# A decode kernel's ring of weight loads: each load of 0.75 or 1 MB issued as two loads, even partitions by SyncE and odd partitions by ScalarE

## The chip, the cores and the metric

The kernel runs on one core of one Trainium2 chip. The metric is device time in microseconds: the median over several executions. The profile is one execution of its own, recorded by the hardware profiler. Its span runs from the first to the last instruction; a little time lies outside the span, so the execution's own time is somewhat longer.

The engines are named as the profile names them: PE is TensorE (PEld its weight loads), ACT is ScalarE, DVE is VectorE, POOL is GpSimd, SP is SyncE. Sixteen DMA engines move data between HBM and the on-chip memory SBUF. A DMA is issued by an engine's instruction queue; those that SP issues appear in the trace as queue q1, those that ACT issues as queue q10.

## The reference

Two kinds of layers alternate, twice: grouped-query attention over a cache, then a dense layer with GELU. There are 8 sequences of one token (B = 8, D = 1024), 32 query heads on 4 key/value heads of size 128, 4096 cache positions, and a hidden size of 3584. Everything is float32, and both attention layers read the same caches and the same weights.

```
def attention(x):
    q = (x @ wq)                                   # 8 x 4096, as 32 heads of 128
    scores = einsum("bhqd,bhkd->bhqk", q, k) * 128 ** -0.5
    o = einsum("bhqk,bhkd->bhqd", softmax(scores), v)
    return o @ wo
def dense(x):
    return gelu(x @ w1 + b1) @ w2 + b2

x = x + attention(layernorm(x))
x = x + dense(layernorm(x))
x = x + attention(layernorm(x))
x = x + dense(layernorm(x))
```

The two caches are 64 MB each (1 MB = 1024 x 1024 bytes here), wq and wo 16 MB each, w1 and w2 14 MB each. With one token per sequence each weight and cache element is used for a few multiplications only, so nearly all of the work is to bring 369 MB (in millions of bytes) from HBM.

## The kernel before

All loads go into one large tile in SBUF, `arena`, 128 partitions of 218 KB each, which the kernel divides by hand into units of 1 KB per partition. A cache tile of 8 units (1 MB over the 128 partitions) is one head and half the positions of one sequence.

**The stream of loads.** Before any computation is written, the kernel fills a list, `stream`, with every load of the program in the order in which the data is needed: its key, its place in the arena, its size in units and its source. `pump` (L183) takes loads from the head of the list as long as the head's place is free, and issues each with one `nc.sync.dma_start` (L190). `give` (L76) marks a place as free and calls `pump`; the computing functions call it as soon as they have written the last instruction that reads a place. So a load stands in SP's queue in the list's order, and at run time SP waits there for the matmuls that read the old contents of its place. A load can't be issued before those ahead of it in the list.

**The stages.** In the first layer the query weights (two loads of 8 MB) and then key and value caches (mostly 8 MB per load, one sequence's keys or values) stream through three areas A, B and C of 64 units each. The second attention layer goes through the sequences backwards. It finds the caches of sequence 7 and the keys of sequence 6 still in place, which saves their loads. The price is that between the two attention layers most of the arena is occupied: output weights `o0`, the dense layer's `i0` and `p0`, and the second layer's query weights `q1` all have to pass through a **ring** of four slots of 8 units, at R[0] to R[3] (L558). Loads there are 1 MB (8 KB per partition); one of `q1` has 6 units (0.75 MB), one has 4, and the last load of `p0` is cut into two of 4 units. After the ring the other caches and the last layer's weights go through the large areas again.

**The work around the ring.** `project` (for o and p) and `expand` (for i and q) loop over the loads of their weight. For each slot they write the matmuls that read it and then call `give`, whose `pump` issues the load that takes the slot next. `layernorm` uses DVE and ACT for the row's statistics: the squares at L167 (ACT), then, some tiles later, the square root at L174 (ACT). Its result is first used at L242 (DVE), where a unit's products are scaled. `hidden_unit` applies GELU with a tanh on ACT (L291). Before the ring begins, ACT copies some pieces out of the way (L628, L630), which frees R[1]; attention's values (L483) free the last slot.

ACT issues one DMA, the input load at the very start (L82). Every other load and the store at the end (L682) are issued by SP.

The instructions of each engine run in the order in which the program writes them; there is no planner that would move them.

Of the kernel before, what the change touches and what calls it, by code (L numbers as in the profile page):

```python
# [14 lines left out]
P = 128  # L15
# [37 lines left out]
def decode_layers(ctx: ExitStack, tc: tile.TileContext, x, kc, vc, wq, wo, w1, w2, w2_low, out):  # L53


    nc = tc.nc
# [12 lines left out]
    def is_free(at, n):  # L69
        return not any(u in used for u in range(at, at + n))  # L70

    def take(at, n, who):
        assert is_free(at, n), (who, at, n)
        used.update(dict.fromkeys(range(at, at + n), who))

    def give(at, n):  # L76
        for u in range(at, at + n):
            used.pop(u)
        pump()
# [99 lines left out]

    stream = []  # L180
    held = {}

    def pump():  # L183
        while stream and is_free(stream[0][1], stream[0][2]):
            key, at, n, src = stream.pop(0)
            take(at, n, key)
            dst = arena[:, at * KB:at * KB + src.shape[1]]
            if key[0] == "low":
                dst = arena[key[1]:LOW:4, AT_LOW * KB:AT_LOW * KB + src.shape[1]]
            nc.sync.dma_start(out=dst, in_=src)  # L190
            held[key] = at, n

    def loads(name):
# [403 lines left out]
    open_queries()  # L597
    rsum = row_sums()
    pump()
    nc.vector.tensor_reduce(rsum, x_row, AX.X, ALU.add)  # L600

# [162 lines left out]
```

## Time and profile before

| | us |
|---|---|
| median of 3 runs | 869.54 (869.48 to 869.60) |
| the profiled execution's own time | 869.43 |
| its span | 867.6 |
| PE, DVE, ACT busy in the span | 541.9, 175.3, 52.9 |

How it is read: the page gives each engine's busy time, and forty slices of the span with the busy share of each engine, the clock granted to PE and what the DMA engines moved. A DMA share of 1.00 means that all 16 DMA engines were occupied by packets for the whole stretch; packets that overlap a little can raise it above 1.00. A packet is one contiguous run of bytes, such as one partition's row of a load; the small packets of 4 bytes are those that report a load's completion. "GB/s" counts millions of bytes per millisecond. The chain is the sequence of work that ended last, followed back from the end, and a wait is put down to what released it.

The cache stage of the first layer lies at about 40 to 340 us, the ring at about 360 to 500 us, and the second attention layer and the last weights follow it.

### The profile page before, as it was taken

The numbers are of one execution on the slowest core, as the hardware profiler recorded it, in microseconds if no ns is written. First come the engines' busy times: TensorE is split into PE (matmuls) and PEld (weight loads), VectorE is DVE, ScalarE is ACT, GpSimd is POOL, SyncE is SP. The second block draws the span as 40 slices with busy tenths as digits, with TensorE's granted clock in tenths as the row PEclk, the third lists the DMA queues.
The fourth block names the chain that finished last, engine by engine and source line by source line (L and its number), as shares of the span: only waits on it lengthen the run. The fifth ranks groups of instructions, "written<-read, shape, count | busy, mean of one in ns | idle before, by whom it ended". The sixth has DMA issues, their size and how long they took to land.

```text
span 867.6 us, 8713 instructions
## 1 busy us (share of the span) xinstructions
PE 541.9 (62%) x3896; PEld 173.1 (20%) x3896; DVE 175.3 (20%) x458; ACT 52.9 (6%) x84; POOL 3.5 (0%) x14
## 2 busy tenths in 40 slices
PE   0556575655656566867676587776574654665677
PEld 0112121211212122221221132222121211211222
DVE  0001231313122232200110023332231313120011
ACT  0200000000000011000000010000000000000100
POOL 0000000000000000000000000000000000000000
PEclk9977787777777877766876888977787777777789
DMA  9999999999999999999999999999999999999997
GB/s 393 436 436 433 435 430 433 435 433 433 435 430 433 435 417 426 407 419 421 420 420 420 421 420 437 438 433 433 435 433 433 435 433 435 433 432 433 420 425 308
DMA packets 16669, 369.06 MB, mean 425 GB/s; under 512 B 1868, under 2 KB 2028, under 8 KB 2924
## 3 DMA queue, kind: packets, MB, share of 16 engines
q1 hardware_dynamic: 16488, 368.36, 99.3%
q8 instruction: 30, 0.49, 0.2%
q10 hardware_dynamic: 144, 0.15, 0.0%
q14 instruction: 7, 0.06, 0.0%
HBM read 368.47 MB, written 0.03 MB: 425 GB/s over the span
## 4 chain that ended last, share of the span: by engine, by line
DMA 77%; PE 20%; DVE 1%; ACT 1%; issue 0%; SPq 0%; POOL 0%; ACTq 0%; POOLq 0%
DMA arena<-in_A_k_cache_dram 22%; DMA arena<-in_A_v_cache_dram 21%; DMA arena<-in_B_w_dram 16%; DMA arena<-in_A_wo_dram 10%; DMA arena<-in_A_wq_dram 8%; PE sps L483 6%; PE sps L426 6%; PE sps L217 2%; PE sps L314 2%; PE sps L497 1%; PE spot L339 1%; PE sps L461 0%; ACT arena L450 0%; DVE arena L434 0%; ACT arena L464 0%
## 5 line engine op out<-in xcount | busy, mean ns | idle before, releaser
L426 PE MATMUL sps<-arena 128*32 128x512 f32 x992 | 142.4, 712 | 116.6 <-DMA arena<-in_A_k_cache_dram 104.4
L483 PE MATMUL sps<-arena 128*32 128x512 f32 x1024 | 151.7, 732 | 19.6 <-DMA arena<-in_A_v_cache_dram 19.6
L217 PE MATMUL sps<-arena,xnT 128*32 128x512 f32 (+3 forms) x592 | 77.0, 650 | 37.3 <-DMA arena<-in_A_wq_dram 19.3
L426 PEld LDWEIGHTS sps<-arena 128*32 128x32 f32 x992 | 31.2, 124 | 192.6 <-DMA arena<-in_A_k_cache_dram 96.8
L314 PE MATMUL sps<-arena,oT 128*32 128x256 f32 x496 | 50.5, 546 | 22.4 <-DMA arena<-in_B_w_dram 10.6
L490 DVE TENSOR_TENSOR sps<-sps,misc 128x512 f32<-128x512 f32 x64 | 44.3, 692 | 65.0 <-PE sps L483 65.0
L461 PE MATMUL sps<-ident,arena 128*128 128x128 f32 x128 | 28.8, 365 | 43.5 <-ACT arena L450 31.6
L483 PEld LDWEIGHTS sps<-arena 128*32 128x32 f32 x1024 | 33.0, 130 | 95.6 <-issue 72.5
L450 ACT ACTIVATE arena<-arena,bias 128x1024 f32<-128x1024 f32 x16 | 18.4, 1147 | 492.2 <-DVE scratch L447 492.2
L434 DVE TENSOR_SCALAR_CACHE_REDUCE arena<-sps 128x512 f32<-128x512 f32 x32 | 22.1, 691 | 124.6 <-PE sps L426 124.6
L491 DVE TENSOR_REDUCE scratch<-sps 128x128 f32<-128x512 f32 x64 | 44.2, 691 | 2.2
L499 DVE TENSOR_TENSOR oT<-sps,scratch 128x8 f32<-128x8 f32 x64 | 11.0, 172 | 160.5 <-PE sps L497 160.5
L217 PEld LDWEIGHTS sps<-arena,xnT 128*32 128x32 f32 x592 | 18.1, 127 | 84.3 <-DMA arena<-in_A_wq_dram 30.3
L497 PEld LDWEIGHTS sps<-misc,scratch 128*128 128x128 f32 x128 | 21.5, 211 | 66.0 <-DVE scratch L491 39.9
L339 PE MATMUL spot<-arena,oT 128*32 128x512 f32 x120 | 16.9, 717 | 18.9 <-DMA arena<-in_A_wo_dram 18.9
L461 PEld LDWEIGHTS sps<-ident,arena 128*128 128x128 f32 x128 | 18.2, 179 | 51.8 <-ACT arena L450 35.5
L497 PE MATMUL sps<-misc,scratch 128*128 128x8 f32 x128 | 27.4, 286 | 1.2 <-DVE scratch L491 1.2
L314 PEld LDWEIGHTS sps<-arena,oT 128*32 128x32 f32 x496 | 17.1, 142 | 53.3 <-DMA arena<-in_A_wo_dram 19.6
L339 PE MATMUL spot<-arena 128*32 128x512 f32 (+2 forms) x108 | 17.9, 682 | 1.8 <-DMA arena<-in_B_w_dram 1.8
L466 DVE COPY arena<-sps 128x512 f32<-128x512 f32 x16 | 11.1, 691 | 37.1 <-PE sps L461 37.1
L156 PE MATMUL sps<-nmean,rsum 128*128 128x64 f32 x8 | 2.0, 336 | 25.3 <-DVE rsum L600 23.7
L468 PE MATMUL sps<-scratch,misc 128*128 128x32 f32 x32 | 10.0, 404 | 12.5 <-DVE arena L466 12.5
(105 smaller groups left out, 163.2 us busy)
## 6 DMA issues: line engine op xcount, KB each, us to landing
arena<-in_B_w_dram SPq DMA_DIRECT2D x27, 1024.0 KB, 8.0
arena<-in_A_wo_dram SPq DMA_DIRECT2D x16, 1024.0 KB, 8.7
arena<-in_A_wq_dram SPq DMA_DIRECT2D x14, 1024.0 KB, 8.7
arena<-in_A_k_cache_dram SPq DMA_DIRECT2D x3, 4096.0 KB, 17.8
arena<-in_A_v_cache_dram SPq DMA_DIRECT2D x3, 4096.0 KB
arena<-in_A_v_cache_dram SPq DMA_DIRECT2D x4, 2048.0 KB, 11.2
arena<-in_B_w_dram SPq DMA_DIRECT2D x1, 6144.0 KB, 45.9
arena<-in_B_w_dram SPq DMA_DIRECT2D x1, 5120.0 KB, 39.4
```

The lines of the kernel that those rows point to most:

```text
L217: nc.tensor.matmul(acc[32 * j:32 * j + 32, r * P:(r + len(ts)) * P], xnT[:, kt * B:kt * B + 32], blocks[:, ts[0] - t0:ts[-1] - t0 + 1:4], ...
L314: nc.tensor.matmul(y[32 * j:32 * j + 32, a:a + n], weights, data, start=(j not in begun), stop=stop)
L339: nc.tensor.matmul(y2[32 * j:32 * j + 32, h * CH:(h + 1) * CH], weights, data, start=((h, j) not in begun2), stop=stop)
L426: nc.tensor.matmul(ps[32 * g:32 * g + 32, :], q[:, c:c + 32], kt[:, g * CH:(g + 1) * CH], start=(j == 0), stop=(j == HKV - 1))
L434: nc.vector.tensor_scalar(row[:, half * CH:(half + 1) * CH], ps, SCALE, None, op0=ALU.mult, op1=ALU.max, accum_out=st["mx"][:, half:half + 1])
L450: nc.scalar.activation(row, row, AF.Exp, bias=bias, scale=1.0, accum_out=ls)
L461: nc.tensor.transpose(pp[:, t * P:(t + 1) * P], row[:, c:c + P], ident)
L466: nc.vector.tensor_copy(s[:, half], src)
L483: nc.tensor.matmul(o[32 * g:32 * g + 32, :], s[:, g], v[:, g * CH:(g + 1) * CH], start=(half == 0), stop=(half == NH - 1))
L490: nc.vector.tensor_tensor(blocks, blocks, sel_t.unsqueeze(2).to_broadcast([P, T, DH]), ALU.mult)
L491: nc.vector.tensor_reduce(r, o.rearrange("p (t d) -> p d t", t=T), AX.X, ALU.add)
L497: nc.tensor.matmul(po[:, 0:REP], scratch[:, a:a + DH], sel_h, start=True, stop=True)
```

## The change

In `pump`, a load whose key belongs to `o0`, `i0`, `p0` or `q1` and that has at least 6 units is now issued as two loads: the 64 even partitions by SP and the 64 odd partitions by ACT. Place, size and order of the loads stay, and so do the computing instructions. ACT's load stands in ACT's queue at the point in the program where `pump` was called. The matmuls that read the slot wait for both halves. Loads of 4 units, the caches and the last layer's weights are issued as before.

```
 
     stream = []
     held = {}
+    HALVED_LOADS = ('o0', ('i0', 0), ('i0', 1), 'p0', ('q1', 0), ('q1', 1))
 
     def pump():
         while stream and is_free(stream[0][1], stream[0][2]):
...
             dst = arena[:, at * KB:at * KB + src.shape[1]]
             if key[0] == "low":
                 dst = arena[key[1]:LOW:4, AT_LOW * KB:AT_LOW * KB + src.shape[1]]
-            nc.sync.dma_start(out=dst, in_=src)
+            if key[0] in HALVED_LOADS and n >= 6:
+                nc.sync.dma_start(out=dst[0:P:2], in_=src[0:P:2])
+                nc.scalar.dma_start(out=dst[1:P:2], in_=src[1:P:2])
+            else:
+                nc.sync.dma_start(out=dst, in_=src)
             held[key] = at, n
```

More of the change, by code (lines that the diff above doesn't have):

```diff
@@ L181, in decode_layers @@
     held = {}
+    HALVED_LOADS = ('o0', ('i0', 0), ('i0', 1), 'p0', ('q1', 0), ('q1', 1))
     def pump():
@@ L189, in pump @@
                 dst = arena[key[1]:LOW:4, AT_LOW * KB:AT_LOW * KB + src.shape[1]]
-            nc.sync.dma_start(out=dst, in_=src)
+            if key[0] in HALVED_LOADS and n >= 6:
+                nc.sync.dma_start(out=dst[0:P:2], in_=src[0:P:2])
+                nc.scalar.dma_start(out=dst[1:P:2], in_=src[1:P:2])
+            else:
+                nc.sync.dma_start(out=dst, in_=src)
             held[key] = at, n
```

## The prediction

> **What bounds the kernel now.** I read the page's slices and DMA part first, to see whether any engine or only the transfers fill the span, then the stages, then the chain inside the ring.
>
> ```profile
> PE 541.9 (62%) x3896; PEld 173.1 (20%) x3896; DVE 175.3 (20%) x458; ACT 52.9 (6%) x84; POOL 3.5 (0%) x14
> ...
> DMA  9999999999999999999999999999999999999997
> GB/s 393 436 436 433 435 430 433 435 433 433 435 430 433 435 417 426 407 419 421 420 420 420 421 420 437 438 433 433 435 433 433 435 433 435 433 432 433 420 425 308
> DMA packets 16669, 369.06 MB, mean 425 GB/s; under 512 B 1868, under 2 KB 2028, under 8 KB 2924
> ...
> q1 hardware_dynamic: 16488, 368.36, 99.3%
> ...
> q10 hardware_dynamic: 144, 0.15, 0.0%
> ...
> DMA 77%; PE 20%; DVE 1%; ACT 1%; issue 0%; SPq 0%; POOL 0%; ACTq 0%; POOLq 0%
> ```
>
> No compute engine is near full, the 16 DMA engines are busy in every slice (99.3% of the span for SP's queue, q1, alone), and DMA is 77% of the chain. ScalarE's queue, q10, carries one small load of 0.15 MB. So time is bytes over rate, and a microsecond won or lost on the DMA engines anywhere before the last load shows at the end. By stages (the columns are busy time by engine, then PE's clock, DMA share, GB/s):
>
> ```profile
> 40.00:340.00 300.00, 181.13 (x1166) 56.06 (x1166) 69.72 (x174) 16.12 (x24) 0.00 (x0) 0.77 1.00 431
> ...
> 360.00:500.00 140.00, 95.49 (x829) 29.63 (x833) 9.32 (x36) 7.49 (x14) 0.16 (x1) 0.72 1.01 418
> ```
>
> The change touches the ring, about 360 to 500 us. Its rate is 418 GB/s against 431 in the cache stage before it, at the same full DMA share. The chain there alternates between a load and the matmuls that read it:
>
> ```profile
> 384.56 8.05 DMA arena<-in_A_wo_dram
> 392.61 0.04 issue
> 392.65 1.98 PE sps L314 x16
> 394.62 0.01 issue
> 394.64 7.92 DMA arena<-in_B_w_dram
> ```
>
> A load is issued when its slot's matmuls end and lands 8 us later, since the loads of the other slots are served first; four slots come round in 10.1 us (384.56 to 394.64), four times the price of a load found below. The chain looks like a round trip, but the queue is never empty, so it is the rate that binds.
>
> **The change part by part.** How many loads are halved, and how long each takes to land:
>
> ```profile
> arena<-in_B_w_dram SPq DMA_DIRECT2D x27, 1024.0 KB, 8.0
> arena<-in_A_wo_dram SPq DMA_DIRECT2D x16, 1024.0 KB, 8.7
> arena<-in_A_wq_dram SPq DMA_DIRECT2D x14, 1024.0 KB, 8.7
> ...
> arena<-in_A_wq_dram SPq DMA_DIRECT2D x1, 768.0 KB, 8.2
> ```
>
> That is 27 + 16 + 14 + 1 = 58 loads. Their bytes, rows and slots stay; each gets a second transfer with its own completion. To price that, the DMA part of four short stretches: 50 us of the ring, 100 us of the cache stage (one row of 64 KB per partition), the output store, and the end of that store.
>
> ```profile
> DMA packets 2887, 21.02 MB, mean 420 GB/s; under 512 B 324, under 2 KB 324, under 8 KB 324
> ...
> q1 hardware_dynamic: 2883, 20.96, 100.9%
> ```
> ```profile
> DMA packets 743, 43.30 MB, mean 433 GB/s; under 512 B 80, under 2 KB 80, under 8 KB 80
> ...
> q1 hardware_dynamic: 740, 43.25, 100.0%
> ```
> ```profile
> DMA  0044940440998490929084405404004000000000
> ...
> DMA packets 48, 0.03 MB, mean 117 GB/s; under 512 B 16, under 2 KB 48, under 8 KB 48
> ...
> q1 hardware_dynamic: 48, 0.03, 37.1%
> ```
> ```profile
> DMA packets 4, 0.00 MB, mean 17 GB/s; under 512 B 3, under 2 KB 4, under 8 KB 4
> ...
> q1 hardware_dynamic: 4, 0.00, 7.6%
> ```
>
> The ring, 400 to 450 us: 20.96 MB are 20 loads of 1.048 MB, so **2.50 us a load**; 2883 packets over 20 are 144, which is 128 partition rows of 8 KB and 16 small ones, one completion on each engine. The store, 866.20 to 866.48 us: 32 rows of 1 KB and 16 small packets take 37.1% of 16 x 0.28 us, 1.66 us. Its end, 866.41 to 866.47: one row and three small take 7.6% of 16 x 0.06 us, 0.073 us. Both together give a small packet 8.4 ns and a 1 KB row 48 ns. **Added work:** 16 small packets over 16 engines, so 8.4 ns a load, 58 x 8.4 ns = **+0.5 us**.
>
> Is there more to a load than its rows? Cache stage, 130 to 230 us: 660 rows of 64 KB in 1600 us of engine time are 2.42 us each, or 303 ns for 8 KB. A ring load has eight rows on each engine; at 303 ns they would take 2.42 us, and it takes 2.50. The 0.08 us is either a price of shorter rows (eight times 10 ns), which halving leaves alone, or of each load, which halving pays again. Both kinds of load have eight rows and one completion per engine, so these rows alone can't tell. Bounds: 58 x 0.08 = **+4.6 us** if it is per transfer, **-4.6 us** if a second queue hides it whole. What I go by is the one stretch with two queues at work, 15.5 to 33.3 us, when ScalarE's input load runs beside the first weights:
>
> ```profile
> DMA packets 192, 7.40 MB, mean 416 GB/s; under 512 B 32, under 2 KB 80, under 8 KB 80
> ...
> q1 hardware_dynamic: 128, 7.34, 95.1%
> q10 hardware_dynamic: 64, 0.06, 0.9%
> ```
>
> Here 48 rows of 1168 bytes and 16 small packets of q10 take 0.9% of 16 x 17.8 us, 2.56 us; less 16 x 8.4 ns that is 51 ns a row. A 1 KB row costs 48 ns with one queue, so a slightly longer row that takes turns with the other queue's costs about what it costs alone: no hiding and no fine. I take 0 for it and keep both ends.
>
> [...]
>
> **The two issuing queues.** SP issues as many transfers as before. ScalarE gets 58 more; the store's issue bounds one at 0.57 us, so under 33 us on an engine that is busy for 52.9 of 867.6.
>
> ```profile
> 865.00 0.57 SPq L682 DMA_DIRECT2D out_dram<-x_all  x1
> ```
>
> Its packets begin at 866.21 (the first non-zero digit of its stretch), 1.2 us after the issue began. A ring load so needs 1.2 + 2.5 = 3.7 us when nothing is in front of it, and has 8.0: ScalarE's half may be issued **4.3 us** late before the engines run dry. What can hold it up, and what stands behind it on ScalarE:
>
> ```profile
> 398.49 0.51 ACT L167 ACTIVATE scratch<-x_all,nmu 128x256 f32<-128x256 f32 x1 [42.01 <-DVE nmu L165]
> ...
> 399.11 1.28 ACT L174 ACT_TABLE_LOAD   x1
> 401.88 0.26 ACT L174 ACTIVATE sd<-sps,misc 128x1 f32<-128x1 f32 x1 [1.49 <-PE sps L152]
> 422.13 1.28 ACT L291 ACT_TABLE_LOAD   x1 [19.99 <-DVE scratch L290]
> 423.43 0.31 ACT L291 ACTIVATE scratch<-scratch 128x128 f32<-128x128 f32 x1
> ```
>
> The long waits (42.0 and 20.0 us) are idle time that had nothing queued; in program order a half stands behind the matmuls that free its slot, and L167, L174 and L291 depend on matmuls of that same order. So a half is late by at most the table load and activation in front of it, 1.28 + 0.31 = 1.6 us, inside 4.3. Turned round, the square root's table load, which now runs in a wait, may come behind two halves and be 1.6 us later. Its reader is the scaling at L242:
>
> ```profile
> L242 DVE TENSOR_SCALAR scratch<-sps,rs 128x512 f32<-128x512 f32 (+1 forms) x3 | 2.1, 706 | 35.2 <-PE sps L217 35.2
> ```
>
> L242 waits 35.2 us for the unit's last matmuls in the ring and for nothing else, so both delays cost 0. Without that cover they would cost 1.6 us at each of the two square roots and two tanhs, 6.4 us. PE now has two completions to wait for per load; the matmuls wait for data anyway (chain above), so 0.
>
> Sum: 869.43 (the profiled execution; span 867.6 and 1.8 around it) + 0.5 = 869.9; the median of the runs lies 0.11 higher, which gives **870.0 us**.
>
> **The rivals.** *ScalarE's halves run ahead.* At the ring's start q10 is empty while SP's queue still holds the last big cache loads, and two queues take turns, so the halves of the first three o0 loads can overtake. Served before older SP halves, three of them (1.25 us each) put a load's landing off by 3.75 us for as long as that lead lasts. That alone fits into 4.3; it decides where ScalarE is late too: 3.75 + 1.6 - 4.3 = 1.05 us dry at each of the four activations, 4.2 us, **874.2**. For it: the turns of the two queues. Against it: the lead shrinks whenever ScalarE is late, and near the end there are no later halves.
>
> *The second queue hides the price of short rows.* While one queue's row ends the other's begins: up to -4.6 us, **864.9**, half of it **867.2**. For it: the ring's 418 against 431. Against: the stretch with two queues shows the full price.
>
> *Two engines share one place in SBUF.* Half the partitions might be dealt to the engines so that two of them write to one group of partitions by turns, each at half its rate: up to 2.50 us more a load, 58 x 2.5 = 145 us, **1015**, and with random phases half, **942**. Against it stands the store, also on a part of the partitions (32, every fourth): with several engines in one slice (digits to 9) its rows took 48 ns, no more than bytes and fixed price; it reads SBUF, though, and is short. [...] No run here shows a load on part of the partitions at length.
>
> *The change does nothing of what it says*, the halves being served as one: that is the forecast less 0.5 us.
>
> **How the numbers follow.** Forecast (with the last case) 0.55, ScalarE's lead 0.20, hidden rows 0.17, shared ports 0.08. A measurement of this kernel can tell 0.2%, 1.7 us, from no change. The forecast lies inside that, the lead and the shared ports are slower, the hidden rows faster: 0.17, 0.56, 0.27 (0.01 of the lead's chance, where it costs too little to be told, goes to no change). The range runs from 866.5, which leaves out hidden rows beyond two thirds, to 875, which takes in the lead and the +4.6 of a price per transfer (874.2) and leaves out the shared ports. The likeliest case alone is 869.5 to 871.
>
> **What would show it.** q10 should go from 144 to 144 + 58 x 80 = 4784 packets, q1 from 16488 to 16488 - 58 x 64 = 12776. The ring should stay at 2.50 to 2.51 us a load and 418 to 420 GB/s at a full DMA share. If it rises towards 430, rows were hidden; if the share falls under 0.98 inside the ring, queues ran dry; if the share stays full and the rate falls far, engines block each other. ScalarE's square roots may move by 1.6 us with no effect on L242. A change of the time with an unchanged ring rate would prove this whole argument wrong.

## The result: 885.6 us, 1.8% slower

| | us | ratio to before, 95% interval |
|---|---|---|
| before, median of the runs beside it | 869.51 (869.43 to 869.60) | |
| changed, median of 4 runs | 885.60 (884.26 to 885.87) | 1.0182 [1.0164, 1.0200] |
| changed, the profiled execution | 885.78, span 883.0 | |

The change costs 16.1 us. The forecast was 870.0 us, the range 866.5 to 875.

The page of the changed kernel, its engines, slices and DMA part:

```profile
PE 539.0 (61%) x3896; PEld 173.8 (20%) x3896; DVE 175.7 (20%) x458; ACT 52.9 (6%) x84; POOL 3.5 (0%) x14
...
DMA  9999999999999999499999999999999999999996
GB/s 386 464 437 425 428 429 428 433 428 449 433 425 428 430 417 425 159 418 415 422 420 419 409 423 435 438 442 431 430 428 431 436 437 436 435 429 433 425 421 281
DMA packets 17599, 369.07 MB, mean 418 GB/s; under 512 B 2797, under 2 KB 2957, under 8 KB 3853
...
q1 hardware_dynamic: 12776, 338.08, 89.5%
q10 hardware_dynamic: 4784, 30.43, 8.3%
```

The engines did the same work, and the packets are those that the prediction counted (12776 and 4784). One slice out of forty stands out: the seventeenth, with a DMA digit of 4 and 159 GB/s. Before, no slice between the first and the last was below 407. The slices around it move as many bytes as ever. So the time was not lost little by little over 58 halved loads, but in one place, about 353 to 375 us, where the ring begins.

The same place by stretches, first of the changed kernel, then of the kernel before (busy time by engine, then PE's clock, DMA share, GB/s):

```profile
340.00:350.00 10.00, 1.40 (x5) 0.81 (x5) 0.73 (x4) 1.24 (x2) 0.00 (x0) 0.61 0.96 406
350.00:360.00 10.00, 1.12 (x4) 0.72 (x4) 0.33 (x1) 1.62 (x3) 0.00 (x0) 0.50 0.51 212
360.00:370.00 10.00, 9.58 (x58) 3.00 (x62) 3.89 (x9) 0.00 (x0) 0.00 (x0) 0.69 0.56 210
370.00:380.00 10.00, 6.14 (x84) 2.90 (x76) 2.79 (x6) 0.59 (x1) 0.00 (x0) 0.99 0.69 252
380.00:400.00 20.00, 13.51 (x124) 4.60 (x128) 0.00 (x0) 0.00 (x0) 0.00 (x0) 0.59 1.02 422
400.00:450.00 50.00, 32.56 (x293) 10.38 (x285) 3.97 (x13) 3.74 (x6) 0.00 (x0) 0.76 1.01 419
450.00:500.00 50.00, 31.51 (x296) 10.76 (x294) 4.27 (x19) 2.43 (x5) 0.16 (x1) 0.79 1.01 415
```
```profile
340.00:350.00 10.00, 6.55 (x30) 2.92 (x34) 1.81 (x7) 2.87 (x5) 0.00 (x0) 0.50 0.96 406
350.00:360.00 10.00, 7.69 (x70) 2.36 (x62) 5.74 (x11) 0.59 (x1) 0.00 (x0) 1.00 1.02 423
360.00:370.00 10.00, 7.35 (x66) 2.79 (x66) 0.17 (x1) 0.00 (x0) 0.00 (x0) 0.66 1.01 393
370.00:380.00 10.00, 7.55 (x64) 2.35 (x64) 0.00 (x0) 0.00 (x0) 0.00 (x0) 0.53 1.01 416
380.00:400.00 20.00, 14.53 (x134) 4.88 (x134) 0.82 (x4) 1.49 (x3) 0.00 (x0) 0.67 1.02 421
400.00:450.00 50.00, 33.78 (x290) 10.36 (x289) 6.00 (x22) 2.53 (x5) 0.16 (x1) 0.71 1.01 420
450.00:500.00 50.00, 32.29 (x278) 9.25 (x280) 2.33 (x10) 3.47 (x7) 0.00 (x0) 0.80 1.01 419
```

From 350 to 380 us the changed kernel moves 2.12 + 2.10 + 2.52 = 6.74 MB, the kernel before 4.23 + 3.93 + 4.16 = 12.32 MB. At 420 GB/s the missing 5.58 MB are **13.3 us**. From 380 to 500 us it falls behind by another 0.23 MB, 0.5 us. Of the 16.35 us between the two profiled executions 2.5 us are left outside these rows: 1.0 of them lies outside the spans (885.78 less 883.0 is 2.8 us, 869.43 less 867.6 was 1.8), the other 1.5 I can't place. Note also the row from 340 to 350 us: the DMA engines still have the cache loads to serve, but PE and DVE have nearly stopped (1.40 and 0.73 us busy; before, 6.55 and 1.81). The DMA engines run dry ten microseconds *after* the compute engines, because places are no longer freed.

Why the compute engines stop stands in the timeline of ScalarE: first the changed kernel, then the kernel before (start, duration, and in brackets the idle time ahead and who ended it).

```profile
315.51 0.52 ACTq L193 DMA_DIRECT2D arena<-in_A_wo_dram  x1
340.94 1.15 ACT L455 ACTIVATE arena<-arena,bias 128x1024 f32<-128x1024 f32 x1 [28.62 <-DVE scratch L452]
...
357.87 0.60 ACT L469 ACTIVATE arena<-sps 128x512 f32<-128x512 f32 x1 [15.69 <-DMA arena<-in_A_wo_dram]
358.36 0.59 ACT L633 COPY sps<-arena 128x512 f32<-128x512 f32 x1
358.88 0.61 ACT L635 COPY arena<-arena 128x512 f32<-128x512 f32 x1
360.44 1.40 ACTq L193 DMA_DIRECT2D arena<-in_A_wo_dram  x2
```
```profile
340.63 1.15 ACT L450 ACTIVATE arena<-arena,bias 128x1024 f32<-128x1024 f32 x1 [29.24 <-DVE scratch L447]
...
343.13 0.60 ACT L464 ACTIVATE arena<-sps 128x512 f32<-128x512 f32 x1 [1.27 <-PE sps L461]
```

L469 (L464 before; the diff moved it by five lines) is the copy of one half of sequence 7's transposed probabilities from `sps` into the place S. It has nothing to do with weights. Yet now it waits 15.69 us for a load of `wo`, and starts 14.7 us later. Behind it in ScalarE's order stand L633 and L635, which free R[1]; R[1]'s load is issued at 360.44. Attention's values, which read what L469 writes, stand still as well.

The load that it waits for is load 0 of `o0`, the first one of the ring and the first that is halved. Its odd half is issued by ScalarE at 315.51; its even half stands in SP's queue behind sequence 7's value loads, and is issued at 327.25 (SP's timeline of the changed kernel):

```profile
320.20 4.66 SPq L195 DMA_DIRECT2D arena<-in_A_v_cache_dram  x4
327.25 51.56 SPq L192 DMA_DIRECT2D arena<-in_A_wo_dram  x8
```

It lands behind 8 MB of values, about 357 us. Before, nobody needed load 0 until PE's first matmuls on it, which start at 358.43.

The wait is in the program. This is the line of L469 in the list of instructions as built, of the changed kernel, with the counters that it waits for; the other one is L464 of the kernel before:

```
L469 ACTIVATE arena<-sps 128x512 [waits DMAHW1_49,PE_49]
L464 ACTIVATE arena<-sps 128x512 [waits PE_49,Activation_49]
```

DMAHW1 counts completions of loads, and both halves of load 0 are counted there. Load 0 goes to R[0], units 184 to 191 of each partition, and L469 writes S, units 212 to 215 (`AT_A, AT_B, AT_C, RING = 0, 64, 128, 184` and `AT_S` = 212). They share no byte. The waits are written by the framework from the access patterns of the instructions. For this pair of patterns it seems to take two separate places for overlapping ones; the run with contiguous halves below tests that. DVE's copy of the other half of S (L471) has the same wait in the list.

### The profile page after: what moved, and what is told of

Same layout as the page of the kernel before. It is cut to its first block, busy times and chain, and to the rows that moved or that the text cites. A ratio compares the mean times of both kernels' runs of the same rounds, so it can differ in the third digit from the quotient of the medians.

```text
span 883.0 us, 8889 instructions
## 1 busy us (share of the span) xinstructions
PE 539.0 (61%) x3896; PEld 173.8 (20%) x3896; DVE 175.7 (20%) x458; ACT 52.9 (6%) x84; POOL 3.5 (0%) x14
## 3 DMA queue, kind: packets, MB, share of 16 engines
q1 hardware_dynamic: 12776, 338.08, 89.5%
q10 hardware_dynamic: 4784, 30.43, 8.3%
## 5 line engine op out<-in xcount | busy, mean ns | idle before, releaser
L431 PE MATMUL sps<-arena 128*32 128x512 f32 x992 | 144.0, 719 | 117.7 <-DMA arena<-in_A_k_cache_dram 105.6
L488 PE MATMUL sps<-arena 128*32 128x512 f32 x1024 | 154.1, 743 | 16.6 <-DMA arena<-in_A_v_cache_dram 16.6
L466 PE MATMUL sps<-ident,arena 128*128 128x128 f32 x128 | 28.6, 363 | 58.2 <-ACT arena L455 31.9
L319 PE MATMUL sps<-arena,oT 128*32 128x256 f32 x496 | 44.4, 489 | 28.2 <-DMA arena<-in_B_w_dram 14.5
L466 PEld LDWEIGHTS sps<-ident,arena 128*128 128x128 f32 x128 | 17.9, 176 | 66.6 <-ACT arena L455 35.7
L471 DVE COPY arena<-sps 128x512 f32<-128x512 f32 x16 | 11.1, 692 | 51.3 <-PE sps L466 51.3
```

The lines of the kernel that those rows point to most:

```text
L319: nc.tensor.matmul(y[32 * j:32 * j + 32, a:a + n], weights, data, start=(j not in begun), stop=stop)
L431: nc.tensor.matmul(ps[32 * g:32 * g + 32, :], q[:, c:c + 32], kt[:, g * CH:(g + 1) * CH], start=(j == 0), stop=(j == HKV - 1))
L466: nc.tensor.transpose(pp[:, t * P:(t + 1) * P], row[:, c:c + P], ident)
L471: nc.vector.tensor_copy(s[:, half], src)
L488: nc.tensor.matmul(o[32 * g:32 * g + 32, :], s[:, g], v[:, g * CH:(g + 1) * CH], start=(half == 0), stop=(half == NH - 1))
```

## The experiments

Four theories were open. **The wait** (W in the expectations): what costs the time is L469's wait for load 0. **The lead** (L): ScalarE's halves are served ahead of older loads of SP and put their landings off, so that the DMA engines run dry. **Halving** (H): each further transfer costs time by itself. **Shared places** (P; "shared ports" in the prediction): halves share places in SBUF and block each other. All diffs are against the changed kernel; no computing instruction was changed in any of them. Each ratio is to the kernel before, run beside it.

### Load 0 whole, the other 57 halved

```
-            if key[0] in HALVED_LOADS and n >= 6:
+            if key[0] in HALVED_LOADS and n >= 6 and key != ('o0', 0):
```

> All ring loads halved as in the change, except the very first one (o0's load 0), which SP issues whole. Theory W: the loss is one added wait, that of the probabilities' copies on ACT and DVE for the landing of the first load's strided halves, late behind the caches in SP's queue. Then no engine waits there, the two dry stretches of the DMA engines near 355 and 367 us vanish, and the time is 869.5 + 0.5 for the completions, 869.5 to 871.5 us. Theory L (ScalarE's halves run ahead of SP's older loads and put landings off): loads 1 to 15 are still halved and still overtake, so 880 us or more. Theory H (halving costs by itself, per transfer): 57 of 58 loads are still halved, 885 us.

Measured: 876.92 us (875.25 to 880.23), ratio 1.0087 [1.0063, 1.0110]. ScalarE's timeline, PE's timeline and the stretches of this kernel:

```profile
342.95 0.60 ACT L469 ACTIVATE arena<-sps 128x512 f32<-128x512 f32 x1 [1.27 <-PE sps L466]
...
345.52 1.17 ACTq L193 DMA_DIRECT2D arena<-in_A_wo_dram  x2
```
```profile
355.70 1.07 PE L488 MATMUL sps<-arena 128*32 128x512 f32 x8 [1.35 <-DMA arena<-in_A_v_cache_dram]
358.10 1.93 PE L488 MATMUL sps<-arena 128*32 128x512 f32 x8 [1.33 <-DMA arena<-in_A_v_cache_dram]
```
```profile
360.00:380.00 20.00, 13.01 (x136) 5.92 (x132) 1.64 (x4) 0.00 (x0) 0.00 (x0) 0.67 0.91 346
...
400.00:450.00 50.00, 33.33 (x262) 10.32 (x266) 6.30 (x23) 4.03 (x7) 0.00 (x0) 0.65 1.00 395
450.00:500.00 50.00, 33.41 (x278) 10.66 (x274) 2.87 (x12) 2.74 (x5) 0.16 (x1) 0.70 1.00 406
```

The wait at L469 is gone and with it more than half of the loss, but 7.3 us stay. Neither theory alone gave that number: the wait would have left 871.5 us at most, the lead 880 or more. Now ScalarE issues at 345.52 into an empty queue, while SP's queue still holds value loads, and the values that PE reads come 1.3 us late at two places. The ring then runs at 346, 395 and 406 GB/s instead of 404 (the mean of 393 and 416), 420 and 419. That is 1.16 + 1.25 + 0.65 = 3.06 MB, or 7.3 us at 420 GB/s: about the whole loss. So the wait is not all that the change does. But the lead explains only a part of this rest. By the share (0.91, 1.00 and 1.00, where the kernel before has 1.01) idle engines account for about 1.2 of the 3.06 MB. The other 1.9 MB were lost while the engines were busy and moved less in the same time; why they did, these runs don't show.

### Load 0 halved, the other 57 whole

```
-            if key[0] in HALVED_LOADS and n >= 6:
+            if key == ('o0', 0):
```

> Only the first ring load (o0's load 0) is halved; the other 57 are whole and SP's. Theory W: the wait of ACT's probability copy for that load's landing is there in full, ACT idle of about 15 us before that copy, two dry stretches, 882 to 886 us. Theory L: one half overtakes at most, 1.25 us, so 869.5 to 871 us. Theory H: a fifty-eighth of the loss, 869.8 us.

Measured: 882.02 us (881.54 to 882.78), ratio 1.0142 [1.0126, 1.0157]. ScalarE's timeline and a stretch:

```profile
357.85 0.60 ACT L469 ACTIVATE arena<-sps 128x512 f32<-128x512 f32 x1 [15.70 <-DMA arena<-in_A_wo_dram]
```
```profile
360.00:380.00 20.00, 15.34 (x138) 5.88 (x138) 6.65 (x14) 0.59 (x1) 0.00 (x0) 0.87 0.66 247
```

One halved load out of 58 brings the same wait, 15.70 us, the same dry DMA engines (share 0.66) and +12.4 us. The other 57 are not needed for it.

### Both halves by SP

```
-                nc.scalar.dma_start(out=dst[1:P:2], in_=src[1:P:2])
+                nc.sync.dma_start(out=dst[1:P:2], in_=src[1:P:2])
```

> Both halves of every one of the 58 loads are issued by SP, even partitions first; ScalarE issues none. Theory W: the halves are strided as in the change, the copies still wait for load 0's landing, 882 to 887 us. Theory L: one queue, so nothing can overtake, 870 us. Theory H: 885 us if the price is of the transfers, 870 if it is of ScalarE's queue.

Measured: 884.73 us (883.99 to 884.80), ratio 1.0170 [1.0155, 1.0185]. ScalarE's timeline:

```profile
357.59 0.60 ACT L469 ACTIVATE arena<-sps 128x512 f32<-128x512 f32 x1 [15.26 <-DMA arena<-in_A_wo_dram]
```

L469 waits 15.26 us for the same load. The second queue is not what makes the wait.

### Both halves by SP, and load 0 whole

The two edits of above together (the first and the third).

> Both halves of every ring load are issued by SP, as in the run with both halves on SP, but o0's load 0 is whole, as in the run with the first load whole. Theory W+L (the added wait on load 0's landing costs about 12 us, and apart from it ScalarE's halves running ahead cost about 7): neither is present, so only 57 more completions are left, 869.5 + 0.5 = 869.5 to 870.5 us, with DMA engines busy through the ring. Theory H (a halved load costs by itself): the 7.3 us of the run with the first load whole remain, 876 us.

Measured: 870.73 us (869.63 to 873.05, 10 runs), ratio 1.0013 [1.0002, 1.0023]. The ring's stretches:

```profile
360.00:380.00 20.00, 14.72 (x130) 5.54 (x130) 0.17 (x1) 0.00 (x0) 0.00 (x0) 0.60 1.00 407
...
400.00:450.00 50.00, 31.29 (x291) 10.22 (x285) 5.52 (x20) 4.02 (x7) 0.16 (x1) 0.78 1.01 413
450.00:500.00 50.00, 32.95 (x290) 10.26 (x286) 2.97 (x13) 4.34 (x7) 0.00 (x0) 0.83 1.02 419
```

57 loads are still made as two, with even and odd partitions. That alone costs 1.2 us (0.2 to 2.0 by the interval of the ratio). Halving by itself is not what costs 16 us. The four kernels make a square:

| median, us | load 0 whole | load 0 halved | the wait costs |
|---|---|---|---|
| both halves in SP's queue | 870.73 | 884.73 | 14.0 |
| one half in each queue | 876.92 | 885.60 | 8.7 |
| the second queue costs | 6.2 | 0.9 | |

Read along its upper row and then down, this is the account of the change: 1.2 us for halving (870.73 less 869.5), 14.0 for the wait, 0.9 for the second queue. The 0.9 can't be told from nothing, since the runs of the two kernels overlap (884.26 to 885.87 and 883.99 to 884.80). Without the wait the second queue costs 6.2 us, so the wait hides it. Why is argued and not shown: behind the wait the DMA engines have run dry (share 0.51 and 0.56), both queues may start level, and ScalarE's lead over SP's old loads is gone. Mending the one alone would have left a good part of the loss.

### Load 0 halved, both halves by ScalarE

```
-            if key[0] in HALVED_LOADS and n >= 6:
-                nc.sync.dma_start(out=dst[0:P:2], in_=src[0:P:2])
+            if key == ('o0', 0):
+                nc.scalar.dma_start(out=dst[0:P:2], in_=src[0:P:2])
```

> Only o0's load 0 is halved into even and odd partitions, and ScalarE issues both halves; all other loads are whole and SP's. The copies of the probabilities wait for both halves in the program, as in the run with only the first load halved, but ScalarE's queue is empty, so both land before the copies are due. Theory W as lateness (it is the landing behind the caches that costs): ACT does not wait there, 869.5 to 871.5 us. If strided halves cost in another way than through that landing: 882 us as with one half on SP.

Measured: 871.48 us (869.83 to 872.86, 10 runs), ratio 1.0020 [1.0011, 1.0030]. ScalarE's timeline:

```profile
315.31 0.52 ACTq L192 DMA_DIRECT2D arena<-in_A_wo_dram  x1
315.87 1.03 ACTq L193 DMA_DIRECT2D arena<-in_A_wo_dram  x1
...
346.33 0.60 ACT L469 ACTIVATE arena<-sps 128x512 f32<-128x512 f32 x1 [1.21 <-PE sps L466]
```

L469 has the wait for load 0's halves in the list of instructions here too, but both are issued before 317 us, in a queue with nothing in front, and have landed when L469 comes: only PE releases it. Of the 12.4 us 2.0 are left, at the upper edge of what was expected. So it is not the wait as such that costs, but that the half it waits for stands behind 8 MB of other loads.

### Load 0 alone halved, but by contiguous partitions

Is it really the pattern that brings the wait? This differs from the second experiment in nothing but which partitions form a half.

```
-            if key[0] in HALVED_LOADS and n >= 6:
-                nc.sync.dma_start(out=dst[0:P:2], in_=src[0:P:2])
-                nc.scalar.dma_start(out=dst[1:P:2], in_=src[1:P:2])
+            if key == ('o0', 0):
+                nc.sync.dma_start(out=dst[0:P // 2], in_=src[0:P // 2])
+                nc.scalar.dma_start(out=dst[P // 2:P], in_=src[P // 2:P])
```

> Only load 0 of o0 is halved, as in the kernel that halves this load alone by even and odd partitions (882.02 us), but by the contiguous partitions 0 to 63 (SP) and 64 to 127 (ScalarE). The same two transfers, the same two queues, the same halves in size; the pattern alone differs. If it is the pattern that makes ScalarE's copy at L469 wait for load 0's landing: no DMA release in front of L469, which starts at 342 to 345 us, and 869.5 to 873 us (one load at 252 instead of 420 GB/s costs about 1.7 us at most). If any halving of load 0 brings that wait, or a ScalarE transfer in front of L469 does: L469 near 357 us and 881 to 884.

Measured: 876.94 us (876.63 to 879.02), ratio 1.0085 [1.0067, 1.0102]. ScalarE's timeline and the stretches:

```profile
346.35 0.60 ACT L469 ACTIVATE arena<-sps 128x512 f32<-128x512 f32 x1 [1.20 <-PE sps L466]
```
```profile
320.00:330.00 10.00, 4.64 (x38) 1.64 (x38) 4.39 (x9) 0.00 (x0) 0.00 (x0) 0.91 0.98 307
...
350.00:360.00 10.00, 9.68 (x60) 2.36 (x52) 4.10 (x8) 0.00 (x0) 0.00 (x0) 0.73 1.02 344
360.00:370.00 10.00, 6.33 (x52) 2.80 (x56) 1.86 (x5) 0.59 (x1) 0.00 (x0) 0.66 0.96 310
```

The wait is gone: L469 is released by PE, and no counter of loads stands beside it in the list. With the same two transfers in the same two queues, the step of two in the partitions is what brings it. Why the framework takes that pattern to reach S is not shown here. The time was outside what I expected (869.5 to 873), for another reason: from 320 to 330 and from 350 to 370 us the rate falls to 307, 344 and 310 GB/s while the engines stay busy (0.98, 1.02 and 0.96). I take these for the stretches in which a contiguous half is served beside whole loads; I had priced only the slowness of the half itself, not that of its neighbours. A part may be ScalarE's half running ahead of cache loads: L469 starts at 346.35 us, 3.2 later than before, as it does at 346.33 in the run with both halves on ScalarE, which cost 2.0 us.

### All 58 halved by contiguous partitions

```
-                nc.sync.dma_start(out=dst[0:P:2], in_=src[0:P:2])
-                nc.scalar.dma_start(out=dst[1:P:2], in_=src[1:P:2])
+                nc.sync.dma_start(out=dst[0:64], in_=src[0:64])
+                nc.scalar.dma_start(out=dst[64:P], in_=src[64:P])
```

> Halves by partitions 0 to 63 (SP) and 64 to 127 (ScalarE) in place of even and odd; count, size, queues and order as in the change. Theory W: the program then holds no wait of the copies for a load, so no dry stretch, 869.5 to 872 us. Theory L: the same overtaking as in the change, 885 us. Theory H: 885 us. Theory P (a half on 64 partitions that lie together shares places in SBUF between engines): the ring's rate falls below 400 GB/s at a full DMA share, 58 loads at up to 5 us each, 900 to 1015 us.

Measured: 969.52 us (962.08 to 971.85), ratio 1.1118 [1.1069, 1.1167]. The ring, 360 to 500 us:

```profile
360.00:500.00 140.00, 71.69 (x515) 22.54 (x511) 8.73 (x28) 4.62 (x8) 0.00 (x0) 0.51 1.00 252
```

The DMA engines are busy all the time (share 1.00) and move 252 GB/s where even and odd halves move 415 to 419: at 252 GB/s a load of 1.048 MB takes 4.16 us in place of 2.50. So the rate falls when halves are cut this way, and not as the change cuts them, as P expected it. Why it falls is not shown, and two halves need not meet for it. In the run above ScalarE's half of load 0, issued at 315.38 us, landed after 14.8 us, and SP's half, issued at 330.21, after 34.3. So of the two only SP's can have been served from 356 to 364 us, and the rate was 238 to 258 GB/s there, at shares of 0.95 to 1.07.

### Loads 0 to 3 whole, and whole loads by turns

Where does the lead come from, and could it be had without halves? First the ring's first round whole, the other 54 loads halved:

```
-            if key[0] in HALVED_LOADS and n >= 6:
+            if key[0] in HALVED_LOADS and n >= 6 and not (key[0] == 'o0' and key[1] < 4):
```

> As the change, but o0's loads 0 to 3, the four that are issued while cache loads still stand in SP's queue, are whole and SP's; the other 54 are halved between SP and ScalarE. Theory L in the form 'the lead is won at the ring's start, over the cache loads': no lead is won there, 869.5 to 871.5 us. Theory L in the form 'a lead is won wherever ScalarE's queue is empty when a half is issued': load 4's half meets an empty queue and overtakes the three whole loads in SP's, the lead stays, and engines run dry where tiles are used late, 874 to 878 us. Theory H: 876 us.

Measured: 874.11 us (873.08 to 875.46), ratio 1.0054 [1.0039, 1.0069]. ScalarE has no halves of loads 1 to 3 here that could meet the value loads, and the median is 2.8 us lower than with load 0 alone whole (the intervals of the two ratios overlap). The rest stays: the ring moves 391 GB/s from 360 to 380 us, 406 from 400 to 450 and 409 from 450 to 500. The cost of the second queue is not tied to the ring's start. The time lies in the range that was expected, but not for the reason given: the share in these stretches is 1.00, 1.00 and 1.01, so the engines did not run dry, they were slower.

Then no halves at all, but odd-numbered loads of the ring whole by ScalarE and even-numbered ones whole by SP:

```
-            if key[0] in HALVED_LOADS and n >= 6:
...
+            on_act = key[0] in HALVED_LOADS and n >= 6 and key[1] % 2 == 1
+            (nc.scalar if on_act else nc.sync).dma_start(out=dst, in_=src)
```

> No load is halved: of each weight in the ring SP issues the even-numbered loads and ScalarE the odd-numbered ones, whole. Theory L: whole loads of ScalarE overtake SP's and are served beside them at half rate each, so a load that is needed first lands later; the lead is up to one load and a half, within the 4.3 us of slack most of the time, 870 to 876 us, with short dry spells. Theory H: nothing is halved, 869.5 us. A shared-rate gain of two queues would show as a ring above 425 GB/s and a time under 868.

Measured: 884.85 us (881.68 to 885.67), ratio 1.0170 [1.0150, 1.0189]: as slow as the change itself, with no added wait at the copy into S (L466 in this kernel). Rows of its chain of waits and two stretches:

```profile
376.37 6.48 DMA arena<-in_A_wo_dram
...
384.03 11.84 DMA arena<-in_A_wo_dram
```
```profile
400.00:450.00 50.00, 29.73 (x269) 9.33 (x267) 5.52 (x20) 4.02 (x7) 0.00 (x0) 0.69 0.97 382
450.00:500.00 50.00, 27.04 (x258) 11.00 (x262) 2.71 (x13) 2.15 (x4) 0.16 (x1) 0.74 0.99 382
```

Loads of one size take 6.48 and 11.84 us from issue to landing, where the chain before shows 8.05 and 7.92. The order of landing is then no longer that of need: PE waits for the late one (up to 5.1 us at a time before L219's matmuls), while the places of those that came early stay full. The ring falls to 382 GB/s. Late landings explain only a part of it: the share, 0.97 and 0.99 against 1.01, would leave 403 and 411 GB/s, and the rest was lost by engines that were busy and slower, as in the kernels before this one. I had expected no more than 876 here, because I took 4.3 us of margin as enough for a lead of one or two loads. It isn't: a load that is put off also puts off the issue of the load that takes its slot, and the margin says nothing of slower engines.

### All 58 halved by columns, both halves by SP

The prediction left open whether the 0.08 us by which a ring load is dearer than its bytes is a price of rows or of transfers. Here the rows are doubled: 128 partitions twice, 4 KB each.

```
-                nc.sync.dma_start(out=dst[0:P:2], in_=src[0:P:2])
-                nc.scalar.dma_start(out=dst[1:P:2], in_=src[1:P:2])
+                h = src.shape[1] // 2
+                nc.sync.dma_start(out=dst[:, 0:h], in_=src[:, 0:h])
+                nc.sync.dma_start(out=dst[:, h:], in_=src[:, h:])
```

> All 58 loads are halved by columns: the same 128 partitions twice, rows of 4 KB instead of 8 KB, both halves issued by SP. There are then 16 rows and 2 completions on each engine per load instead of 8 and 1. If the 0.08 us by which a ring load is dearer than its bytes is a price of each row (10 ns), a load costs another 0.08 us: 58 x 0.08 = 4.6 us, 874 to 875 us, and a ring rate near 408 GB/s. If it is a price of each load or of the stretch, and not of rows, the rate stays at 420 and the time at 869.5 to 871.

Measured: 873.87 us (873.75 to 873.94), ratio 1.0042 [1.0027, 1.0057]. The DMA part of 400 to 450 us:

```profile
DMA packets 5573, 20.32 MB, mean 406 GB/s; under 512 B 620, under 2 KB 620, under 8 KB 5570
...
q1 hardware_dynamic: 5570, 20.28, 102.3%
```

20.28 MB in 50 us are 2.585 us a load, 0.085 more than before, for eight more rows and one more completion on each engine. Less 8.4 ns for the completion that is 9.6 ns a row, and the prediction had put a row at 10. It is a price of rows, so halves by partition don't pay it. The time, 3.5 us above the kernel before it (2.3 to 5.0 by the interval), is a little under the 4.9 that 58 times 0.085 would give.

## Why the prediction was wrong

**The bound held.** The time is set by the DMA engines, and an idle microsecond there shows at the end: 13.8 of the 16.35 us are bytes not moved before 500 us. "The queue is never empty" was true of the kernel before and not of the changed one, which is what the share under 0.98 was named for: it fell to 0.51.

**The terms for the work added held.** The packets came out as counted. The ring, once it runs, moves 419 and 415 GB/s against 420 and 419. Sixteen small packets a load were put at +0.5 us; halving without the wait and the second queue measures +1.2 (0.2 to 2.0). The 0.08 us was rightly left at 0: it is a price of rows, as the kernel with doubled rows shows. The end of +4.6 us is excluded by the kernel that halves in one queue, that of -4.6 by the ring of the changed kernel, where two queues move no more than one.

**The step that failed** is the list of waits: "in program order a half stands behind the matmuls that free its slot" and "PE now has two completions to wait for per load ... so 0". I took the waits that the change adds to be those that the code says, of readers on their data. The framework writes them from access patterns, and the new pattern added one at L469, an instruction that neither reads nor overwrites load 0. It has a price of 14.0 us in one queue and of 8.7 us with two, and the sum had no term for it. The rows for pricing it were there: load 0 is issued last, behind sequence 7's values, and lands late (about 357 us in the changed kernel), and S is written at 343 us; whoever waits for the one before the other is 14 us late. What I lacked was the wait itself, and asking which other instruction names the same tile.

**ScalarE's place in the order held** in the changed kernel. Its square root still comes between two batches of halves, and later than before; the ring's rate from 400 to 450 us is 419, and L247 (L242 before) waits for PE's last matmuls alone (32.4 of the 32.5 us of its waits from 360 to 520 us):

```profile
416.22 1.28 ACT L174 ACT_TABLE_LOAD   x1 [2.69 <-PE sps L152]
...
417.91 15.91 ACTq L193 DMA_DIRECT2D arena<-in_B_w_dram  x7
```

**The rivals.** *ScalarE's halves run ahead*, 874.2 us, named a real cost of the second queue. With the wait out of the way that queue costs 6.2 us, 876.9 in all; that the two numbers are near is partly luck. The term that was off is the margin: 3.75 us of lead "alone fits into 4.3". The lead first met the value loads, which have no such margin (PE waits 1.35 and 1.33 us there). The rate does fall near ScalarE's activations (334 GB/s from 405 to 407.5 us and 329 from 480 to 485, in the kernel with load 0 whole), but also where there is none (315 from 420 to 422), and mostly with busy engines (0.94, 0.97 and 0.90), not dry ones as the rival had it. In the change itself the second queue costs 0.9 us, if anything. *Hidden rows*: with both queues at work the changed ring moves 422 GB/s at best (380 to 400 us), where one queue moved 421, so nothing is hidden. *Shared ports*: the rate falls when halves are cut another way (252 GB/s), not as in this change (419 and 415); contiguous halves cost 100 us, even and odd ones 1.2 with all other costs of halving. That engines take turns at one place in SBUF, at half rate each, was my assumption, and no run shows it; it allowed up to 2.50 us more a load, and contiguous halves took 1.66 more. The guess for random phases was 942, and contiguous halves measured 969.5.

The range missed because its upper end was built from prices per load. The case "a wait elsewhere that the change brings along" was not among the rivals, and it was larger than any that were.

## What to carry to other kernels

Before a transfer's shape is changed, list the waits of the built program and compare them line by line: a framework that finds dependencies from access patterns can take a strided place for a larger one, and the price is not that of the transfer but that of whatever stands behind the new wait. Price such a wait by asking when the thing waited for lands, and where in its queue it stands. In a ring whose slots are freed in order, keep the loads in one queue: a second one brought no byte here, and without the wait it cost 6.2 us with halves and 15.3 with whole loads. And if a load must be cut by partitions, interleave the parts: 57 loads in even and odd halves cost 1.2 us here in one queue, 58 in contiguous halves 100 us in two.

## What the runs showed of the hardware

Three things I had not expected. A single load of 1 MB in two contiguous halves cost 6.6 us, over twice its own 2.50 us; the rate was 307 to 344 GB/s over three stretches of 10 us, so whole loads were slowed too. A DMA share of 1.00 does not mean full rate: it stood at 1.00 with 252 GB/s in the ring of contiguous halves and with 395 GB/s in the kernel with load 0 whole (400 to 450 us), so the GB/s column has to be read beside the share. And two queues are no neutral place for transfers of one order: with whole loads, the same bytes and no further wait, taking turns cost 15.3 us, in part by late landings and in part by busy engines that moved less, for a reason that stays open. How the two queues shared the engines stands in the trace of the changed kernel: from 420 to 470 us q1 takes 50.8% of the time of the 16 DMA engines and q10 50.5%, at 421 GB/s in all.
